# A fused H3 mixer and token MLP: one quarter of the sine table transposed earlier, and a new hand order behind the first shuffles

## The chip, the core and the metric

The kernel runs on one NeuronCore of a Trainium2 chip. The core has five engines that run side by side: TensorE (PE, matmuls and transposes into PSUM), ScalarE (ACT), VectorE (DVE), GpSimd (POOL) and SyncE (SP, which here only issues DMAs). 16 DMA engines move data between HBM and the on-chip memory and within it. The metric is the device time of one execution, in microseconds.

## What is computed

Two blocks follow each other on x = A_q (2048 rows of 448). Cut to what matters:

```
k_shift = sum over t of k_pad[:, t:t+S, :] * shift_k[:, 3-t]      # a filter of 4 taps
kv = k_shift * v
y  = irfft(rfft(kv, 2S) * rfft(ssm_k, 2S))[:S] + kv * ssm_D        # a long causal convolution
h  = x + layernorm(x) * y
u  = gelu(einsum("bsd,sf->bdf", layernorm(h), w1) + b1)            # an MLP along the sequence
h2 = h + (einsum("bdf,fs->bds", u, w2) + b2).transpose(0, 2, 1)
```

Inputs and output are bfloat16. S = 2048, D = 448, F = 1792.

## The kernel before

Every step is recorded first (`op(...)`: its engine, its function, what it reads and writes), with a name `step.number:k`. Nothing is planned at run time or by a heuristic: the strings in `ORDER` list, for each engine, all of its operations in the order in which they run, and `SLOTS` lists for every PSUM buffer which of the eight banks it takes and in which turn. `schedule()` replays these lists, and `emit()` writes the instructions with the semaphore waits that follow from data and buffers. An engine runs its list strictly in order, so an operation that waits holds up all that stand behind it.

The convolution is done as a transform of two stages with matmuls against tables of sines.

- `tables` builds the tables. `tables.5` and `tables.6` hold the phases of the halves h = 0 and h = 1 of the sine table E (DVE: L834, L838, L841) and their sine on ACT (L844). `tables.7` builds the small tables of stage 2 and of the inverse (sine L859 on ACT, products on POOL, L868). E has four quarters of eight 128x128 blocks.
- `kv` is the filter of 4 taps: transposes of k (L962), matmuls (L988), and the product with v (DVE, L1003). `kT` transposes the long filter ssm_k (L1034, evacuated at L738 by DVE); between its groups stand a few dummy matmuls (L1021), which compute nothing.
- `k1`, `u1` (`emit_stage1`) are stage 1 of the filter and of kv: for each of 16 pieces 8 matmuls (L1055), one evacuation of 128x896 (L1065 on ACT or DVE; for the first four pieces of k1 L1063 on DVE), and after every second piece three shuffles between partitions by DMA (L1071), one from SP and two from POOL. They go out of a ring of four buffers.
- `k2`, `u2` (`emit_stage2`) are stage 2 (L1090), evacuated by L736 and L739 (filter) or L735 and L738 (kv). `evac` is the helper of all evacuations: L735 and L736 are its lines on ACT, L738 and L739 on DVE.
- `i1` is the product of the two spectra (DVE, L1157) and the first stage of the inverse (L1174), in eight pairs of pieces, each with two evacuations (L735 or L738) and up to four shuffles by DMA (L1198; L1185 for the last pair). Names: `i1.1`, `i1.14`, `i1.8`, `i1.10`, `i1.12`, `i1.6`, `i1.4`, `i1.16` are the pairs in the order in which they run.
- `ct0` and `ct` transpose the sine table E for the second stage of the inverse: eight transposes per quarter (L1104) and one evacuation of 128x1024 into ET. `ct0.0` is quarter 0, and its `safter=i1_last[-1:]` names the last i1 matmul recorded so far, so it stands amid i1. `ct0.1` is a set of small DMAs on SP that need it: two fill rows with zeros (L1114), four copy rows of ET into a table EW (L1123). `ct.0` to `ct.2` are the other quarters, behind i1.
- `i2` is the second stage of the inverse (L1300 for two rows from EW, L1306), then the gate and the combination with x (ACT L1316, DVE L1318, L1326, L1336), and the second layer norm (ACT L1354, POOL L1364 to L1378, DVE L1385). `q` and `xn` are the first layer norm (DVE L1234, L1236; POOL L1242, L1245; ACT L1267).
- `warm` are single matmuls (L1208) without use for the result.
- `mlp` is the MLP: L1432 and L1442 with w1, the gelu (ACT L1422), L1454 with w2, and the last sum (DVE L1457). `w1a`, `w1b`, `w2` are its weight loads on SP (L1405, L1409, L1416); from the second on they wait until the i1 shuffles have landed.

Of the kernel before, what the change touches and what calls it, by code (L numbers as in the profile page):

```python
# [36 lines left out]
    ),  # L37
    "act": (
# [536 lines left out]
def _build(nc, A_q, A_k, A_v, A_shift_k, A_ssm_k, A_ssm_D, B_w1, B_b1, B_w2, B_b2, out):  # L575
# [33 lines left out]
    o_E = o_V + 14336  # L609
# [13 lines left out]
    o_IH = o_ID + 256  # L623
# [6 lines left out]
    with ctx:  # L630
# [395 lines left out]
        def emit_kT():  # L1026
            k = None
            for i, c in enumerate((0, 1, 2, 3)):
                cw = CW[c]
                for g in range(2):  # L1030
                    sch.t0 = T_KT + 1.0 * (2 * i + g)
                    b = _Buf(psum)
                    for rr in range(8):
# [3 lines left out]
                            safter=(k,) if c == 3 and rr == 0 else ())  # L1037
# [4 lines left out]
                if i < 3:  # L1042
                    dummy(N_WK, T_KT + 1.0 * (2 * i + 1), (k,))
# [100 lines left out]
        i1_last = []  # L1144
# [372 lines left out]
```

## Time and profile before

| | us |
|---|---|
| median of three runs | 171.09 |
| lowest and highest | 170.84, 171.63 |
| the profiled execution | 173.72 |
| its span, first to last instruction | 171.8 |

| engine | busy, us |
|---|---|
| PE | 162.3 |
| DVE | 101.7 |
| ACT | 90.5 |
| POOL | 59.7 |

The profile is of a single execution, and its times count from its first instruction. A row of the timeline gives the start, the length, the engine, the line, the operation, output and input with their shapes, and how many were merged; in brackets stands the idle time of the engine before it and what ended that. A row of the chain of work that ended last gives the start, the length, and the engine or transfer that the end hung on at that time. A row of a group of instructions gives the count, the busy time in us, the mean of one in ns, and the idle time before them. Rows with SPq and POOL of DMA_DIRECT2D show the issuing of a DMA, not the transfer.

### The profile page before, as it was taken

What the parts mean: (1) busy time and instruction counts of PE and PEld (TensorE: products, weight loads), DVE (VectorE), ACT (ScalarE), POOL (GpSimd) and SP (SyncE); (2) the same over time, 40 slices, a digit from 0 to 9 for tenths busy, and PEclk for the clock granted to TensorE, in tenths of its full rate; (3) what the DMA queues carried; (4) which work ended last, traced back from release to release, by engine and by line L of the source; (5) the groups of instructions that cost most, each with busy time, mean ns of one, the idle gap of its engine ahead of it and who ended that gap; (6) DMA issues with size and microseconds to landing.
All of it is one profiled execution on the core that took longest, in us unless ns stands there. A gap on an engine that the chain in (4) does not pass through costs nothing.

```text
span 171.8 us, 3572 instructions
## 1 busy us (share of the span) xinstructions
PE 162.3 (94%) x1419; PEld 94.5 (55%) x1419; DVE 101.7 (59%) x190; ACT 90.5 (53%) x131; POOL 59.7 (35%) x155
## 2 busy tenths in 40 slices
PE   6999999989988998959999999999999999999994
PEld 2786755443323343424544555555567777777783
DVE  7999998989999999948977830000003133132231
ACT  3696858999999999948875371203180000000000
POOL 8345727775910556752887370000000000000000
PEclk9999999999999999987999999999999999999999
DMA  5999798882849387658999999910000111101111
GB/s 161 414 342 369 228 299 327 341 322 110 255 106 391 100 232 203 185 147 276 387 398 402 424 422 421 420 67 0 0 0 4 53 53 53 53 0 57 53 53 53
DMA packets 15564, 35.15 MB, mean 205 GB/s; under 512 B 3804, under 2 KB 9644, under 8 KB 15548
## 3 DMA queue, kind: packets, MB, share of 16 engines
q1 hardware_dynamic: 12396, 28.26, 44.9%
q0 software_dynamic: 3008, 6.58, 12.5%
q8 instruction: 11, 0.18, 0.4%
q10 hardware_dynamic: 144, 0.08, 0.2%
q14 instruction: 5, 0.04, 0.1%
HBM read 22.05 MB, written 1.84 MB: 139 GB/s over the span
## 4 chain that ended last, share of the span: by engine, by line
PE 68%; ACT 21%; DMA 6%; DVE 2%; issue 2%; POOL 0%; DVEq 0%; ACTq 0%
PE ps L1454 24%; PE ps L1432 12%; PE ps L1442 12%; ACT arena L735 12%; DMA arena<-arena 6%; ACT arena L1065 6%; PE ps L1306 3%; PE ps L1055 3%; PE ps L1021 3%; ACT arena L736 3%; PE ps L962 3%; PE ps L1090 2%; PE ps L1034 2%; DVE arena L1336 1%; PE ps L988 1%
## 5 line engine op out<-in xcount | busy, mean ns | idle before, releaser
L1457 DVE SCALAR_TENSOR_TENSOR arena<-ps,arena 128x448 bf16<-128x448 f32 (+2 forms) x17 | 11.1, 656 | 55.3 <-PE ps L1454 55.3
L1454 PE MATMUL ps<-arena 128*128 128x448 bf16 (+2 forms) x238 | 42.7, 342 | 0.0
L1454 PEld LDWEIGHTS ps<-arena 128*128 128x128 bf16 x238 | 33.3, 145 | 9.5
L735 ACT CAST arena<-ps 128x896 bf16<-128x896 f32 (+1 forms) x30 | 23.8, 968 | 0.6 <-PE ps L931 0.4
L1432 PE MATMUL ps<-arena 128*128 128x448 bf16 x112 | 23.4, 353 | 0.1
L1065 ACT CAST arena<-ps 128x896 bf16<-128x896 f32 x25 | 21.0, 919 | 4.5 <-PE ps L1055 4.4
L1442 PE MATMUL ps<-arena 128*128 128x448 bf16 x112 | 22.2, 352 | 0.0
L1071 POOL DMA_DIRECT2D arena<-arena x32 | 17.6, 556 | 9.5 <-ACT arena L1065 8.3
L1422 ACT ACTIVATE arena<-ps,arena 128x448 bf16<-128x448 f32 x14 | 7.8, 641 | 18.3 <-PE ps L1442 14.6
L1090 PE MATMUL ps<-arena 128*64 128x448 bf16 x128 | 15.3, 359 | 2.2 <-ACT arena L735 0.7
L1432 PEld LDWEIGHTS ps<-arena 128*128 128x128 bf16 x112 | 10.8, 98 | 10.8 <-DVE arena L1385 0.9
L1157 DVE TENSOR_TENSOR arena<-arena 128x1792 bf16<-128x1792 bf16 x16 | 16.6, 1082 | 0.1
L1442 PEld LDWEIGHTS ps<-arena 128*128 128x128 bf16 x112 | 11.0, 98 | 10.2
L1055 PE MATMUL ps<-arena 128*32 128x448 bf16 x256 | 14.7, 356 | 0.5 <-ACT arena L1065 0.2
L1174 PE MATMUL ps<-arena 64*128 64x448 bf16 x128 | 13.7, 351 | 0.9 <-DVE arena L1157 0.6
L1198 POOL DMA_DIRECT2D arena<-arena x16 | 9.3, 585 | 14.5 <-ACT arena L735 11.9
L1090 PEld LDWEIGHTS ps<-arena 128*64 128x64 f16 x128 | 5.6, 108 | 11.3 <-ACT arena L735 4.5
L1385 DVE TENSOR_SCALAR arena<-arena 128x448 bf16<-128x448 f32 x16 | 7.9, 510 | 5.2 <-POOL arena L1378 5.1
L1306 PE MATMUL ps<-arena 128*128 128x448 bf16 x32 | 8.7, 395 | 2.0 <-DMA arena<-arena 2.0
L1174 PEld LDWEIGHTS ps<-arena 64*128 64x128 f16 x128 | 5.3, 94 | 8.8 <-DVE arena L1157 3.0
L1354 ACT ACTIVATE arena<-arena 128x448 bf16<-128x448 f32 x14 | 8.0, 573 | 4.0 <-DVE arena L1326 3.8
L1003 DVE TENSOR_TENSOR arena<-ps,arena 128x512 bf16<-128x512 f32 (+1 forms) x16 | 9.1, 614 | 1.0 <-PE ps L988 0.8
(99 smaller groups left out, 191.3 us busy)
## 6 DMA issues: line engine op xcount, KB each, us to landing
arena<-in_B_w_dram SPq DMA_DIRECT2D x8, 896.0 KB, 9.6
arena<-in_B_w_dram SPq DMA_DIRECT2D x2, 2048.0 KB, 17.4
arena<-arena SPq DMA_DIRECT2D x16, 224.0 KB, 3.8
arena<-arena POOLq DMA_DIRECT2D x32, 112.0 KB, 3.9
arena<-in_B_w_dram SPq DMA_DIRECT2D x2, 1536.0 KB, 19.3
arena<-arena POOLq DMA_DIRECT2D x13, 196.0 KB, 4.6
arena<-in_A_k_dram SPq DMA_DIRECT2D x4, 448.0 KB, 5.7
arena<-in_A_v_dram SPq DMA_DIRECT2D x4, 448.0 KB, 8.2
```

Of the source, the lines that this page charges most:

```text
L735: return e.copy(out=dst(), in_=src())
L1055: op("pe", lambda e, W, b=b, r=r, q=q, x=x, c0=c0: e.matmul(PS[32 * q:32 * q + 32, b.slots[x], 0:D], E[:, 2 * r + x, c0:c0 + 32], src[:, r ...
L1065: return e.copy(out=dst, in_=Ppair(b)) if W == "act" else e.tensor_copy(out=dst, in_=Ppair(b))
L1071: shuf[tag].append(op(q_, lambda e, W, g=g, i=i, a=a, nu=nu, jh=jh: e.dma_start(T[a + i:a + i + 4 * nu - 3:4].rearrange("p (j k) c d -> p ...
L1090: op("pe", lambda e, W, b=bs[h], h=h, j=j, c=c, par=par: e.matmul(PS[64 * par:64 * par + 64, b.slots[c], 0:D], FW[:, 64 * c:64 * c + 64], ...
L1157: op("dve", lambda e, W, m=m, i=i: e.tensor_tensor(out=MR(m.slots[0]).rearrange("p (x y) d -> p x y d", x=2), in0=TU[:, i].unsqueeze(2).br ...
L1174: k = op("pe", lambda e, W, b=bs[h], m=ms[h], par=par, t=t, tab=tab, xy=xy, P=P: e.matmul(Pb(b, par), tab[P, :], MR(m.slots[0])[P, xy, :], ...
L1306: k = op("pe", lambda e, W, b=b, r=r, h=h: e.matmul(Pb(b), ET[:, 2 * r + h, :], TZ[:, r, h, :], start=(h == 0 and r >= NZ), stop=(h == 1)) ...
L1432: op("pe", lambda e, W, r=r, fc=fc, b=bs[fc]: e.matmul(Pb(b), W1A[:, r, 128 * fc:128 * fc + 128], Q[:, r, :], start=(r == 0), stop=(r == R ...
L1442: op("pe", lambda e, W, r=r, fc=fc, b=b: e.matmul(Pb(b), W1B[:, r, 128 * (fc - n0):128 * (fc - n0) + 128], Q[:, r, :], start=(r == 0), sto ...
L1454: op("pe", lambda e, W, r=r, fc=fc, b=b, d0=d0, d1=d1: e.matmul(Pb(b)[:, d0:d1], W2[fc // 7][:, fc % 7, r:S:R], G[:, fc, d0:d1], start=(fc ...
L1457: op("dve", lambda e, W, r=r, b=b, A=A, d0=d0, d1=d1: e.scalar_tensor_tensor(out=XR(r)[:, d0:d1], in0=Pb(b)[:, d0:d1], scalar=bm[:, r:r + ...
```

## The change

The transposes of quarter 0 lose the edge to the last i1 matmul, so the order may put them anywhere behind the sine. They now stand amid the transposes of ssm_k (`kT`), in the place of three dummy matmuls, and are evacuated by ACT instead of DVE; on ACT the sine of the half h = 0 goes ahead of that of h = 1, and the copy goes ahead of the small sine of `tables.7`. The strings for all engines are new from there on: up to the first shuffles of k1 they differ in little, behind them in much. On SP the four copies into EW (`ct0.1:2` to `ct0.1:5`) stand ahead of all i1 shuffles, and both zero fills ahead of the loads of x. A number of evacuations change between ACT and DVE, and most PSUM buffers get another bank. The computed result is the same.

```
                 for i in range(8):
                     op("pe", lambda e, W, b=b, h=h, i=i: e.transpose(
...
-                       r=[...], bw=[b], kind="tr", safter=i1_last[-1:])
+                       r=[...], bw=[b], kind="tr", safter=i1_last[-1:] if late else ())
...
-                if i < 3:
+                if i < 2:
                     dummy(N_WK, T_KT + 1.0 * (2 * i + 1), (k,))
...
     "pe":
-        "... kT.2:0-3 kT.3:9-11 kT.5:0-7 kT.2:4-7 kT.5:9-10 kT.6:0-7 kT.7:0-7 bias.0:0 kT.5:11 kv.7:0-7 k1.8:0-7 "
+        "... kT.2:0-3 kT.3:9-11 kT.5:0-7 kT.2:4-7 ct0.0:0-7 kT.6:0-7 kT.7:0-7 bias.0:0 kv.7:0-7 k1.8:0-7 ..."
...
-        "... u1.2:0-7 u1.3:0-7 kv.13:8-27 u1.4:0-7 k1.5:0-7 kv.14:0-23 k1.6:0-7 u1.5:0-7 k1.2:0-7 k1.7:0-7 ..."
+        "... u1.2:0-7 u1.3:0-7 u1.4:0-7 kv.13:0-27 k1.5:0-7 k1.6:0-7 kv.14:0-23 k1.7:0-7 k1.2:0-7 u1.5:0-7 ..."
...
-        "... u2.10:0-3 i1.1:1-8 i1.14:10-17 i1.1:10-17 i1.14:1-8 i1.8:1-8 i1.10:1-8 i1.8:10-17 i1.10:10-17 u2.4:0-3 u2.5:0-3 ct0.0:0-7 i1.12:1-8 ..."
+        "... i1.1:1-8 i1.1:10-17 u2.10:0-3 i1.14:1-8 i1.14:10-17 i1.10:1-8 i1.8:1-8 i1.8:10-17 u2.4:0-3 u2.5:0-3 i1.10:10-17 ..."
...
-        "i1.16:1-8 ct.0:0-7 ct.1:0-7 i2.1:0-3 warm.0:0 i2.9:0-3 i2.2:0-1 i2.10:0-1 ct.2:0-7 warm.1:0 i2.45:0-1 ..."
+        "i1.16:1-8 ct.0:0-7 warm.0:0 i2.1:0-3 ct.1:0-7 i2.9:0-3 i2.2:0-1 i2.10:0-1 ct.2:0-7 i2.45:0-1 ... i2.32:0-1 warm.1:0 "
...
     "act":
-        "tables.0:5 kv.4:12 kv.3:8 kv.6:12 tables.6:3 tables.5:3 tables.7:5 bias.0:1 k1.8:8 ..."
+        "tables.0:5 kv.4:12 kv.3:8 kv.6:12 tables.5:3 tables.6:3 ct0.0:8 bias.0:1 tables.7:5 k1.8:8 ..."
...
-        "... u1.0:8 u1.1:8 u1.2:8 u1.3:8 u1.4:8 k1.5:8 k1.6:8 u1.5:8 k1.7:8 ..."
+        "... u1.0:8 u1.1:8 u1.2:8 u1.4:8 k1.5:8 k1.6:8 k1.7:8 u1.5:8 ..."
...
     "dve":
-        "... i1.0:0 i1.14:0 i1.1:0 i1.7:0 i1.13:0 i1.9:0 i1.8:0 i1.10:0 i1.11:0 i1.10:9 i1.12:0 ct0.0:8 i1.5:0 ..."
+        "... i1.0:0 i1.1:0 i1.13:0 i1.14:0 i1.9:0 i1.7:0 i1.8:0 i1.10:0 i1.12:0 i1.11:0 i1.10:18 ... i1.5:0 i1.6:0 i1.3:0 i1.6:9 ..."
...
     "sp":
-        "u1.11:11 u1.15:11 ct0.1:0 xload.2:0 xload.3:0 w1a.0:0 ct0.1:1 i1.1:20 i1.1:22 i1.14:20 i1.14:22 i1.8:20 "
-        "i1.8:22 i1.10:20 i1.10:22 ct0.1:2 ct0.1:4 i1.12:20 i1.12:22 ct0.1:3 ct0.1:5 i1.6:22 i1.4:18 i1.16:21 "
-        "i1.16:19 w1a.1:0 ..."
+        "u1.11:11 u1.15:11 ct0.1:0-1 xload.2:0 xload.3:0 w1a.0:0 ct0.1:2 ct0.1:4 ct0.1:3 ct0.1:5 i1.1:20 i1.1:22 "
+        "i1.14:20 i1.14:22 i1.8:20 i1.8:22 i1.10:20 i1.10:22 i1.12:20 i1.12:22 i1.6:22 i1.4:18 i1.16:21 i1.16:19 "
+        "w1a.1:0 ..."
```

In these strings `...` stands for names that are left out. In a group of i1 such as `i1.10`, `:1-8` and `:10-17` are the matmuls of its two halves, `:9` and `:18` their evacuations, and the numbers from 19 on its shuffles.

More of the change, by code (lines that the diff above doesn't have):

```diff
@@ L1105, in emit_ct @@
                         out=Pbf(b, 0, f16)[:, 128 * i:128 * i + 128], in_=E[:, 8 * h + i, :], identity=IH),
-                       r=[(o_E + 2048 * h + 256 * i, 256), (o_IH, 256)], bw=[b], kind="tr", safter=i1_last[-1:])
+                       r=[(o_E + 2048 * h + 256 * i, 256), (o_IH, 256)], bw=[b], kind="tr", safter=i1_last[-1:] if late else ())
                 evac(lambda h=h: ET[:, 8 * h:8 * h + 8, :].rearrange("p a b -> p (a b)"),
```

134 rows, old and new, of tables (ORDER, SLOTS) are left out of this document.

## The prediction

> **What bounds the kernel now.** I read the engine shares first, then the table of stages, then the chain of work that ended last.
>
> ```profile
> PE 162.3 (94%) x1419; PEld 94.5 (55%) x1419; DVE 101.7 (59%) x190; ACT 90.5 (53%) x131; POOL 59.7 (35%) x155
> ...
> PE 68%; ACT 21%; DMA 6%; DVE 2%; issue 2%; POOL 0%; DVEq 0%; ACTq 0%
> ```
> ```profile
> 30.00:40.00 10.00, 8.81 (x152) 4.54 (x148) 9.32 (x19) 9.45 (x13) 6.97 (x14) 1.00 0.88 332
> 40.00:50.00 10.00, 9.25 (x106) 3.20 (x100) 9.81 (x16) 9.61 (x12) 6.68 (x15) 1.00 0.49 142
> 50.00:60.00 10.00, 9.18 (x88) 3.26 (x85) 9.95 (x11) 10.00 (x14) 2.39 (x4) 1.00 0.66 222
> 60.00:70.00 10.00, 9.33 (x92) 3.93 (x92) 9.87 (x12) 10.00 (x13) 5.27 (x10) 1.00 0.80 217
> ...
> 75.40:81.40 6.00, 5.89 (x28) 3.00 (x28) 4.64 (x14) 3.30 (x6) 1.24 (x3) 0.72 0.61 197
> 81.40:127.00 45.60, 45.60 (x240) 23.38 (x241) 16.39 (x47) 21.17 (x48) 15.09 (x38) 1.00 0.70 279
> ```
> ```profile
> 66.95 2.45 ACT arena L735 x3
> 69.40 0.04 issue
> 69.44 0.81 ACT arena L735
> 70.25 5.13 DMA arena<-arena
> ...
> 75.42 1.48 PE ps L1306 x4
> ...
> 82.51 0.38 PE ps L1306 x2
> ...
> 126.83 42.08 PE ps L1454 x231
> ```
>
> The share of 94% for PE is misleading. In the table (window, length, then busy time of PE, weight loads, DVE, ACT and POOL, granted clock, DMA share, GB/s) PE is really full only from 81.4 us on: 45.60 of 45.60, then the 42.08 us of the last chain row. None of the products there is removed, so the change is worth exactly what it moves the point at 81.4. Ahead of it, from 50 to 70 us, ACT is busy 10.00 of 10.00 twice and DVE 9.95 and 9.87. They empty PSUM and form the products of the spectra. The chain agrees: ACT evacuations up to 70.25, then 5.13 us of a shuffle through the DMA engines, and only then the first matmul that reads the shuffled rows.
>
> **The transposes of quarter 0 (ct0.0), early.** They leave the full stage and go among the filter's transposes.
>
> ```profile
> 7.20 1.22 DVE L841 TENSOR_SCALAR arena<-arena 128x2048 int32<-128x2048 int32 x1
> ...
> 11.71 0.54 PE L1021 MATMUL ps<-arena 128*128 128x448 bf16 x2
> ...
> 35.10 1.70 PE L1090 MATMUL ps<-arena 128*64 128x448 bf16 x16 [0.59 <-ACT arena L1065]
> ...
> 60.47 0.62 PE L1104 MATMUL ps<-arena 128*128 128x128 f16 x8
> ```
> ```profile
> 8.72 3.91 ACT L844 ACTIVATE arena<-arena 128x2048 f16<-128x2048 int32 x2
> 12.53 0.61 ACT L859 ACTIVATE arena<-arena 128x384 f32<-128x384 int32 x1
> 13.51 0.17 ACT L735 CAST arena<-ps 128x14 f32<-128x14 bf16 x1 [0.38 <-PE ps L931]
> 14.76 1.71 ACT L1065 CAST arena<-ps 128x896 bf16<-128x896 f32 x2 [1.08 <-PE ps L1055]
> ```
>
> Can the input be late? The two sines (L844) change places, so that the half with quarter 0 comes first. Its argument is ready when the second L841 ends, at 7.20 + 1.22 = 8.42 us, and ACT starts its first sine at 8.72 anyway. So the first sine ends near 8.72 + 3.91/2 = 10.7 us, and PE arrives at the new place at about 11.7. No wait. On PE, eight transposes (0.62 us as a burst at the old place) replace three dummy matmuls, two of which take 0.54 us here: about 0 us. On ACT the copy of 128x1024 is a new piece of about 0.9 to 1.0 us between the sines and L859. ACT has 0.38 + 1.08 = 1.46 us idle between the bias and the first evacuation at 14.76, so this fits, with about 0.5 us over. Without that cover the first four evacuations would slip by up to 1.0 us. What stands behind it, the small sine L859 and POOL's tables made from it, comes some 1 us later; stage 2 (L1090), which reads them, starts at 35.10. I cost the early part at 0, between 0 and +0.5.
>
> **The evacuations between 18 and 71 us.** Of the evacuations that carry 896 columns, seven go from ACT to DVE (u1.3, u1.15, one each of k2.1, u2.1, u2.13, i1.10, i1.6) and six from DVE to ACT (u1.11, one each of k2.1, k2.15, u2.1, i1.10, i1.12): ACT has one less, DVE one more, and DVE loses the copy of quarter 0.
>
> ```profile
> L735 ACT CAST arena<-ps 128x896 bf16<-128x896 f32 x29 | 23.6, 996 | 0.2 <-PE ps L1090 0.2
> ...
> L739 DVE TENSOR_SCALAR arena<-ps 128x896 bf16<-128x896 f32 x7 | 7.3, 1082 | 0.7 <-PE ps L1090 0.7
> ...
> L738 DVE COPY arena<-ps 128x1024 f16<-128x1024 f16 x1 | 0.7, 692 | 0.1
> ```
>
> In a stream an ACT evacuation costs 23.6/29 = 0.81 us, a DVE one 7.3/7 = 1.04, the copy 0.69. So ACT: -0.81. DVE: +1.04 - 0.69 = +0.35. DVE's idle time from 30 to 70 us is 0.68 + 0.19 + 0.05 + 0.13 = 1.05, which can take the 0.35 if it lies in the right places; if all of it can be used, the end moves by -0.81, and if none, DVE is the longer one and the end moves by +0.35. Shared evenly over both engines it is (0.35 - 0.81)/2 = -0.23. ACT is the engine in the chain, so I take a value on its side of the middle: **-0.4**, with both ends kept. PE loses 0.62 us of transposes at 60 us, where it is busy 9.33 of 10 and waits for the other two: 0.
>
> The rest of the reordering (kv.13 behind u1.4, each i1 pair finished before the next is begun) changes who waits within the stage and removes no work. Its first shuffles leave earlier, but the later pairs set the end. It is inside the bounds above.
>
> **SP's queue.** The four small copies into EW (L1123) no longer stand between the i1 shuffles; they go ahead of all of them, behind the zero fill and the loads.
>
> ```profile
> 64.11 1.66 SPq L1123 DMA_DIRECT2D arena<-arena  x2
> 65.86 1.41 SPq L1198 DMA_DIRECT2D arena<-arena  x2
> 67.32 2.16 SPq L1123 DMA_DIRECT2D arena<-arena  x2
> 69.52 1.43 SPq L1198 DMA_DIRECT2D arena<-arena  x2
> 70.99 1.39 SPq L1185 DMA_DIRECT2D arena<-arena  x2
> 76.81 1.47 SPq L1405 DMA_DIRECT2D arena<-in_B_w_dram  x3
> ```
> ```profile
> 65.35 5.94 ACT L735 CAST arena<-ps 128x896 bf16<-128x896 f32 x7
> ```
> ```profile
> 69.93 1.15 POOL L1198 DMA_DIRECT2D arena<-arena  x2 [1.54 <-ACT arena L735]
> 71.07 0.61 POOL L1185 DMA_DIRECT2D arena<-arena  x1
> 71.67 0.55 POOL L1198 DMA_DIRECT2D arena<-arena  x1
> 72.21 0.61 POOL L1185 DMA_DIRECT2D arena<-arena  x1
> ```
>
> The pair of L1123 at 67.32 holds SP until 69.48, and from there SP issues four shuffles back to back, one each 0.7 us. The second of them (near 70.23) belongs to the same pair as POOL's at 69.93, so it is at least 0.3 us late. ACT's last evacuation ends at 65.35 + 5.94 = 71.29, and SP's last shuffle goes out near 70.99 + 0.70 = 71.7: 0.4 us late. These delays go. But POOL's last, at 72.21, is the later one of the two, it is not behind L1123, and the weight load that waits for the shuffles starts at 76.81. So of 0.4 us I take **-0.1** (bounds 0 and -0.4). Moving the copies forward puts the first i1 shuffles of SP behind them; those carry the two last rows, which nothing reads before 75 us, so I cost that at 0.
>
> The Trainium skill speaks against more than this ("DMA: Bandwidth & Descriptors", section "Issuing engines are not separate DMA queues"): copies started by any engine run on the same 16 DMA engines, so another issuer saves only issue time. By it the freed SP is worth the 0.4 us of issue at most, and nothing of the 5.13 us.
>
> **Sum.** 0 - 0.4 - 0.1 = -0.5 us. The profiled execution took 173.72 us, 171.8 of it the span and 1.9 around it; it becomes 173.2. The median of the runs, 171.09, lies 2.6 below the profiled one; I subtract the same 0.5 there: **170.6 us**.
>
> Part of those 2.6 us is the clock: 0.72 from 75.4 to 81.4 us means (1 - 0.72) x 6.0/0.5 = 3.4 us at half speed, and four matmuls took 1.48 us at 75.42, where two take 0.38 later. The change has the same gap ahead of them, so I count no difference. The Trainium skill's "TensorE: Matmul & The Clock Gate" (Part 1, "What's actually happening") states half clock after an idle window of about 3.4 us whose phase is free; the 3.4 us here agree, and a kernel could therefore show the dip in one run and not in another.
>
> **Rivals.**
> *More than the sum.* The whole ACT evacuation is gained and SP's lateness too: -0.81 - 0.41 = -1.2, 169.9 us. For it: the second line of the first fence, where ACT has 21% of the chain and DVE 2%. Against it: DVE is as full as ACT.
> *DVE becomes the bound.* The change does not do what it says: the copy leaves, but a longer evacuation comes, and ten products in a row hold up others. +0.35 - 0.1 = about +0.2, 171.3 us. For it 9.95 and 9.87 of 10.00; against it the 1.05 us of idle time.
> *The last shuffles crowd each other (slower).* SP's and POOL's last shuffles now leave closer together.
>
> ```profile
> arena<-arena POOLq DMA_DIRECT2D x2, 196.0 KB, 5.7
> ```
> ```profile
> arena<-arena POOLq DMA_DIRECT2D x1, 98.0 KB, 4.6
> arena<-arena POOLq DMA_DIRECT2D x1, 28.0 KB, 4.5
> ```
>
> The first row is of the issues at 61.4 us, where SP and POOL issue as fast as they can: 5.7 us to landing. The others are of the last ones, near 72 us: 4.6. If the end gets as crowded, the last landing comes 5.7 - 4.6 = 1.1 us later; if the pair before it, which the first matmul behind the gap reads, is stretched as well, up to twice that. In the middle it is +1.65, less the 0.4 of the evacuations: +1.2, 172.3 us (bounds 171.8 and 172.9). It decides as soon as the last shuffle takes more than 5.0 us, and ends beyond 171.95 when it takes some 5.9. For it: the DMA share is 0.80 from 60 to 70 us. Against it: the bytes are the same and the first pairs leave earlier.
>
> **How the numbers follow.** Chances: the sum 0.40, more than the sum 0.31, DVE 0.11, crowding 0.18. Half a per cent, about what a measurement of this kernel can tell from no change, is 0.86 us: faster means below 170.23, slower above 171.95. The sum and DVE lie within; of the sum 0.03 may reach below 170.23. Of the crowding 0.03 lies under 171.95, and about as much comes from an early slip (+0.5) met with DVE's +0.35. That gives faster 0.34, same 0.48, slower 0.18. The forecast's own range is 170.2 to 171.0; the range for eight in ten goes from 169.6 (a little beyond the full gain) to 172.0 (the lower part of the crowding).
>
> **What would show it.** Right: the copy of 128x1024 on ACT ends before 14.3 us and the first L1065 stays near 14.7; ACT's last evacuation ahead of the late transposes ends at 70.9 instead of 71.29; SP issues its last shuffle within 0.1 us of that; the last POOL shuffle goes out near 71.8 and takes about 4.6 us; the back-to-back stretch begins 0.5 us earlier than 81.4. Wrong: DVE without any idle time and ACT waiting in the stage; a last landing of 5.5 us or more; or a start of the stretch that moves because the granted clock dips in one of the two profiles and not in the other.

## The result and the profile after

| | before | changed |
|---|---|---|
| median of the runs | 171.92 us (170.84 to 172.84, 20 runs) | 171.02 us (170.21 to 171.78, 20 runs) |
| profiled execution | 173.72 us, span 171.8 | 171.1 us, span 169.1 |

The ratio is 0.9941, 95% interval [0.9924, 0.9959]: some 1.0 us faster, where 0.5 was forecast. In this series the kernel before took 171.92 us, in the three runs shown ahead of the prediction, the first of these 20, 171.09, so only the ratio is to be compared.

The two profiled executions differ by more than the medians, 2.6 us. The first rows to read are therefore span and mean granted clock, of the execution shown before and of a second profile of the same unchanged kernel (`before_again` below):

```profile
core 0: 171.8 us, clock 0.988
```
```profile
core 0: 169.9 us, clock 1.000
```

The execution shown before was a rare one. Of 95 other runs of that kernel one had a clock as low (0.990, 174.12 us), and all others 0.998 or more. PE's gap ahead of `i2.2`, the first matmul that needs the late shuffles, was longer in it as well, 2.01 us where the second profile has 0.95:

```profile
75.42 1.48 PE L1306 MATMUL ps<-arena 128*128 128x448 bf16 x4 [2.01 <-DMA arena<-arena]
```
```profile
74.43 0.93 PE L1306 MATMUL ps<-arena 128*128 128x448 bf16 x4 [0.95 <-DMA arena<-arena]
```

From here on the second profile stands for the kernel before. Its chain of waits, start and length in us:

```profile
70.11 4.27 DMA arena<-arena
74.38 0.05 issue
74.43 0.93 PE ps L1306 x4
75.36 0.24 PE ps L1104 x4
75.62 0.68 DVE arena L1336
76.29 0.55 DVE arena L1342
76.84 0.93 PE ps L1306 x4
...
79.72 1.12 PE ps L1432 x5
...
124.98 42.09 PE ps L1454 x231
```

The changed kernel, same view:

```profile
71.52 4.20 DMA arena<-arena
75.77 2.82 PE ps L1306 x14
...
124.11 42.09 PE ps L1454 x231
```

In the old chain the end hangs on a shuffle issued at 70.11. It is SP's half of the seventh pair (`i1.4:18`; the expectations below count from 0 and call it the sixth), not one of the last pair: the first matmul behind the gap (`i2.2`, 74.43) needs it, and behind that matmul a product (L1336) and its statistics (L1342) on DVE hold up the next rows until 76.84. By the trace's records of DMA the last shuffle of all landed shortly before, at 76.64, and it was SP's; POOL's last landed at 75.94. In the new chain it hangs on POOL's last shuffle, issued at 71.52. PE's own rows of the changed kernel there:

```profile
73.52 0.92 PE L1306 MATMUL ps<-arena 128*128 128x448 bf16 x4 [0.61 <-issue]
74.27 0.61 PE L1104 MATMUL ps<-arena 128*128 128x128 f16 x8
75.77 1.50 PE L1306 MATMUL ps<-arena 128*128 128x448 bf16 x7 [0.89 <-DMA arena<-arena]
...
78.67 1.12 PE L1432 MATMUL ps<-arena 128*128 128x448 bf16 x5
```

`i2.2` comes 0.9 us sooner than in the kernel before (0.4 us when both are counted from the last evacuation), PE then waits for the transfer and not for DVE, and from 75.77 on it runs without a gap.

The table of stages of the changed kernel (window, length, busy time of PE, weight loads, DVE, ACT and POOL, granted clock, DMA share, GB/s):

```profile
30.00:40.00 10.00, 9.33 (x152) 4.32 (x156) 9.90 (x18) 9.12 (x11) 6.84 (x13) 1.00 0.85 316
40.00:50.00 10.00, 9.12 (x104) 3.11 (x96) 9.61 (x14) 9.78 (x13) 6.17 (x14) 1.00 0.52 145
50.00:60.00 10.00, 9.39 (x86) 3.18 (x84) 9.96 (x10) 10.00 (x14) 2.87 (x5) 1.00 0.81 266
60.00:70.00 10.00, 9.29 (x90) 3.58 (x87) 9.78 (x17) 9.95 (x14) 5.48 (x11) 1.00 0.64 197
...
78.70:124.30 45.60, 45.60 (x241) 23.38 (x241) 16.55 (x47) 21.70 (x48) 14.02 (x38) 1.00 0.74 293
```

The stretch is as full as before (45.60 of 45.60, then 42.09), and ACT is as full from 50 to 70 us as it was. The DMA share has turned round: 0.66 and 0.80 before from 50 and from 60 us, now 0.81 and 0.64. The transfers come earlier.

ACT's last evacuations, before (second profile) and now:

```profile
63.71 7.53 ACT L735 CAST arena<-ps 128x896 bf16<-128x896 f32 x9
```
```profile
12.27 0.99 ACT L735 COPY arena<-ps 128x1024 f16<-128x1024 f16 x1
...
14.18 1.71 ACT L1065 CAST arena<-ps 128x896 bf16<-128x896 f32 x2 [0.33 <-PE ps L1055]
...
63.18 7.53 ACT L735 CAST arena<-ps 128x896 bf16<-128x896 f32 x9
```

They end at 71.24 and at 70.71. From there to the stretch it takes 79.72 - 71.24 = 8.48 us and 78.67 - 70.71 = 7.96 us. So of the 1.05 us between the two starts of the stretch 0.53 lie ahead of the last evacuation and 0.52 behind it. (From its start to the first L1454 the stretch takes 45.26 us before and 45.44 now, so 0.87 of the 1.05 us reach the end.) Of the first part only 0.18 can be put down to the change: from the first evacuation of `k2.3` (43.66 and 43.32) to the end of the last one it takes 27.58 and 27.40 us, and the place where that begins scatters from 43.3 to 44.2 over eleven profiles, with no order by kernel. The rows of ACT there, before (second profile) and now, show one wait for PE fewer:

```profile
45.67 1.76 ACT L736 ACTIVATE arena<-ps 128x896 bf16<-128x896 f32 x2 [0.20 <-PE ps L1090]
47.62 0.91 ACT L735 CAST arena<-ps 128x896 bf16<-128x896 f32 x1 [0.19 <-PE ps L1090]
```
```profile
45.33 2.54 ACT L736 ACTIVATE arena<-ps 128x896 bf16<-128x896 f32 x3 [0.23 <-PE ps L1090]
47.75 0.91 ACT L735 CAST arena<-ps 128x896 bf16<-128x896 f32 x1
```

SP's issues in the changed kernel:

```profile
50.78 2.68 SPq L1123 DMA_DIRECT2D arena<-arena  x4
54.39 15.26 SPq L1198 DMA_DIRECT2D arena<-arena  x12
69.79 1.62 SPq L1185 DMA_DIRECT2D arena<-arena  x2
```

The four copies (L1123) are through before the first shuffle, and SP ends its last issue at 71.41, 0.7 us after the last evacuation: it issues without delay and is no longer in the chain, which is POOL's.

### The profile page after: what moved, and what is told of

The parts are those of the page before. It is cut to its first block, busy times and chain, and to the rows that moved or that the text cites. A ratio compares the mean times of both kernels' runs of the same rounds, so it can differ in the third digit from the quotient of the medians.

```text
span 169.1 us, 3564 instructions
## 1 busy us (share of the span) xinstructions
PE 160.0 (95%) x1416; PEld 92.3 (55%) x1416; DVE 101.9 (60%) x191; ACT 90.5 (54%) x130; POOL 58.5 (35%) x155
## 4 chain that ended last, share of the span: by engine, by line
PE 64%; ACT 19%; DMA 5%; DVE 4%; POOL 4%; issue 2%; DVEq 0%; ACTq 0%; POOLq 0%
PE ps L1454 25%; PE ps L1432 13%; PE ps L1442 13%; ACT arena L735 12%; DMA arena<-arena 5%; ACT arena L736 4%; ACT arena L1065 4%; PE ps L1306 3%; PE ps L1055 3%; PE ps L1034 2%; PE ps L988 2%; PE ps L1090 2%; POOL arena L1071 2%; DVE arena L834 1%; PE ps L962 1%
## 5 line engine op out<-in xcount | busy, mean ns | idle before, releaser
L1454 PE MATMUL ps<-arena 128*128 128x448 bf16 (+2 forms) x238 | 42.7, 342 | 0.0
L1454 PEld LDWEIGHTS ps<-arena 128*128 128x128 bf16 x238 | 33.3, 145 | 9.5
L1432 PE MATMUL ps<-arena 128*128 128x448 bf16 x112 | 23.5, 353 | 0.0
L735 ACT CAST arena<-ps 128x896 bf16<-128x896 f32 (+1 forms) x29 | 23.1, 937 | 0.0
L1065 ACT CAST arena<-ps 128x896 bf16<-128x896 f32 x24 | 20.3, 914 | 4.7 <-PE ps L1055 4.2
L1442 PE MATMUL ps<-arena 128*128 128x448 bf16 x112 | 22.3, 352 | 0.0
L1198 POOL DMA_DIRECT2D arena<-arena x16 | 9.3, 583 | 13.9 <-ACT arena L735 12.9
L1234 DVE BATCH_NORM_STATS2 arena<-arena 128x6 f32<-128x448 bf16 x16 | 9.4, 612 | 0.6 <-DMA arena<-in_A_q_dram 0.6
L1055 PEld LDWEIGHTS ps<-arena 128*32 128x32 f16 x256 | 5.0, 95 | 8.2 <-ACT arena L1065 2.2
```

The lines of the kernel that those rows point to most:

```text
L735: return e.copy(out=dst(), in_=src())
L1055: op("pe", lambda e, W, b=b, r=r, q=q, x=x, c0=c0: e.matmul(PS[32 * q:32 * q + 32, b.slots[x], 0:D], E[:, 2 * r + x, c0:c0 + 32], src[:, r ...
L1065: return e.copy(out=dst, in_=Ppair(b)) if W == "act" else e.tensor_copy(out=dst, in_=Ppair(b))
L1234: op("dve", lambda e, W, bs=bs, r=r: e.bn_stats(out=bs, in_=XR(r)), r=[(oX(r), DB)], w=[(ob, 24)], n=D, kind="1x")
L1432: op("pe", lambda e, W, r=r, fc=fc, b=bs[fc]: e.matmul(Pb(b), W1A[:, r, 128 * fc:128 * fc + 128], Q[:, r, :], start=(r == 0), stop=(r == R ...
L1442: op("pe", lambda e, W, r=r, fc=fc, b=b: e.matmul(Pb(b), W1B[:, r, 128 * (fc - n0):128 * (fc - n0) + 128], Q[:, r, :], start=(r == 0), sto ...
```

## The experiments

Ratios are against the kernel before, run on the same chip in the same series (its medians there: 171.78, 171.90 and 172.01 us). "Back" is the order from matmul `k2.2` on, "front" what stands ahead of it behind the transposes of quarter 0. The last two columns come from one profile each: the longest landing of the shuffles that POOL issues at L1198, and the time from the end of the last evacuation to the stretch. The first four rows come from one series and the last three from another. Two profiles of the changed kernel differ by 0.23 us in the last column (7.96 above, 7.73 here), so a difference of that size tells nothing there.

| kernel | ct0.0 | SP's order | front | back | median us (runs) | ratio | longest landing | to the stretch |
|---|---|---|---|---|---|---|---|---|
| before_again | late | old | old | old | 172.07 (12) | 1.0010 [0.9983, 1.0037] | 5.7 | 8.48 |
| ct0_early | early | old | old | old | 171.61 (12) | 0.9996 [0.9968, 1.0025] | 6.0 | 8.21 |
| ct0_early_sp | early | new | old | old | 171.42 (12) | 0.9970 [0.9941, 0.9998] | 5.6 | 7.79 |
| new_order_old_sp | early | old | new | new | 170.94 (12) | 0.9948 [0.9919, 0.9977] | 4.3 | 7.49 |
| new_back_only | early | new | old | new | 170.74 (10) | 0.9935 [0.9912, 0.9959] | 4.6 | 7.56 |
| new_front_only | early | new | new | old | 171.03 (12) | 0.9956 [0.9936, 0.9976] | 5.8 | 7.95 |
| changed_again | early | new | new | new | 170.86 (10) | 0.9948 [0.9930, 0.9966] | 4.4 | 7.73 |

**The kernel before, once more.**

> The kernel before, unchanged, to see its granted clock run by run. Clock theory (its half-speed dip near 75 us is what the change removes): a good part of the runs show a mean clock of 0.99 or less, and those are about 1 us longer than the others. Shuffle theory (the gain is in the shuffles that land earlier): the clock is 1.00 in nearly all runs, as in the changed kernel, and the span of such runs lies about 1.0 us above the changed kernel's.

The stretch began at 79.72 at full clock, and nearly every run of the unchanged kernel was without a dip. That the change removes a dip falls as a cause.

**Quarter 0 early, and nothing else.**

```
-                       r=[...], bw=[b], kind="tr", safter=i1_last[-1:])
+                       r=[...], bw=[b], kind="tr", safter=i1_last[-1:] if late else ())
...
pe:  -kT.5:9-11                          +ct0.0:0-7 ahead of kT.6:0
act: -tables.6:3 tables.5:3 tables.7:5 bias.0:1    +tables.5:3 tables.6:3 ct0.0:8 bias.0:1 tables.7:5
dve: -ct0.0:8
```

> The kernel before with quarter 0 alone moved: transposes amid those of ssm_k, copy on ACT, nothing else reordered, SP's order as before. Evacuation theory (the full ACT and DVE stage is what got shorter): -0.3 to -0.6 us, since DVE loses its 0.69 us copy. Shuffle theory: -0.2 to +0.1 us, since SP still issues the four copies into EW between the i1 shuffles.

By the runs nothing, 0.9996, but the interval reaches down to what the evacuation theory expected. The trace decides: from `k2.3` to the end of the last evacuation it took 27.56 us instead of 27.58, although DVE no longer has the copy. The evacuation stage is not shortened by that copy.

**SP's new order as well.**

```
sp: -... i1.10:22 ct0.1:2 ct0.1:4 i1.12:20 i1.12:22 ct0.1:3 ct0.1:5 i1.6:22 ...
    +... w1a.0:0 ct0.1:2 ct0.1:4 ct0.1:3 ct0.1:5 i1.1:20 i1.1:22 ...
```

> As ct0_early, and SP's order from the changed kernel: the four copies into EW ahead of all i1 shuffles, both zero fills ahead of the loads of x. Shuffle theory: at least 0.5 us faster than ct0_early, -0.6 to -1.0 us in all, with SP's last large shuffle landing at least 1 us earlier against the last evacuation. Evacuation theory: no more than 0.1 us faster than ct0_early.

By the medians 0.2 us, by the ratios 0.4 against `ct0_early`; the intervals overlap, so if it is a gain it is a small one. By the values neither theory was met: the one asked for 0.5 us at least, the other for no more than 0.1. The chain of `ct0_early`, with the old SP, still goes through the seventh pair's shuffle:

```profile
70.17 4.47 DMA arena<-arena
74.64 0.05 issue
74.69 0.93 PE ps L1306 x4
```

With the new SP order that shuffle went out at 69.85 and landed after 3.35 us by the trace's records of DMA, at 73.20. But POOL's half of the same pair landed at 74.21, so `i2.2` came at 74.30: the other half of the pair took over the wait after 0.4 us. So SP's half did land 1.5 us earlier, counted from the last evacuation, but it was not alone in holding up `i2.2`.

**The changed kernel with SP's old order.**

```
sp: the string of before, all else as changed
```

> The changed kernel with SP's order of before: the four copies into EW between the i1 shuffles again. Shuffle theory: most of the gain goes, -0.4 to +0.1 us against the kernel before. Evacuation theory: -0.7 to -1.0 us, as the changed kernel.

The version of the shuffle theory that rested on SP's queue alone falls: 0.9948, as good as the changed kernel. The time is the one that the evacuation theory expected, but its stage was only 0.17 us shorter than in `ct0_early` (27.39 and 27.56), and the stretch began 0.7 us sooner after it (7.49 and 8.21). The rows of SP show why the copies did no harm.

```profile
63.70 1.35 SPq L1123 DMA_DIRECT2D arena<-arena  x2
65.10 1.41 SPq L1198 DMA_DIRECT2D arena<-arena  x2
66.55 1.34 SPq L1123 DMA_DIRECT2D arena<-arena  x2
67.99 2.51 SPq L1198 DMA_DIRECT2D arena<-arena  x2
```

The copies (L1123) still stand between the shuffles, but the pairs ahead of them now leave earlier, and SP is through with the copies at 67.89. The shuffle at 67.99 is done with at some 68.7, and the seventh pair's goes out as soon as its evacuation is ready (69.81). SP's half then took 3.31 us to land, as with the copies moved. By the ratios the copies cost some 0.3% behind the old pairs, with intervals that overlap, and nothing that can be told behind the new ones.

**Front and back taken apart.** What remained was the order itself. In the new back, the first i1 pair is evacuated ahead of `u2.11`, and each pair is finished before the next is begun. The back also holds a new order of the transposes `ct`, of i2 and of the MLP, which no run takes apart from the pairs.

```
act, old back: u2.7:4 u2.11:5 u2.11:4 i1.1:9 u2.7:5 i1.1:18 i1.14:18 i1.14:9 i1.8:9 i1.8:18 i1.10:18 ...
act, new back: u2.7:4-5 i1.1:9 i1.1:18 u2.11:4 i1.14:9 i1.14:18 u2.11:5 i1.8:9 i1.8:18 i1.10:9 ...
```

> The kernel before with quarter 0 early, SP's new order, and the changed kernel's order from the second last group of the k2 stage (matmul k2.2) on; the k1 and u1 stages keep the old order. Spacing theory (the last half microsecond of the gain comes because the first pair of the i1 stage is evacuated ahead of the last evacuations of the u2 stage, so that the shuffles leave earlier and further apart and land sooner): first shuffle issued 11.1 us after the start of the evacuation stage rather than 13.0; large shuffles 3.8 to 3.9 us in the mean, those of pair 3 (i1.10) 2.5 to 4.2 us; median 171.0 to 171.2, like the changed kernel. Rival, the front order (k1, u1 and the first part of k2): shuffles as above or not, but median 171.4 as with quarter 0 early and SP's new order alone.

> The changed kernel with the old order from matmul k2.2 on (quarter 0 early and SP's new order kept). Spacing theory: pair 3's shuffles 5.5 to 6 us again, large shuffles 4.4 us in the mean, median 171.4 to 171.5. Front rival: 171.0 to 171.1, with the shuffles as slow as before.

> The changed kernel as it is, on the same chip as the three others: 171.0 (170.8 to 171.2), large shuffles 3.8 to 3.9 us in the mean, stretch 7.5 to 8.0 us after the last evacuation.

The shuffles follow the back, as the spacing theory has it. The shuffles of L1198 in the kernel before, `new_front_only` and `new_back_only` (first and last start, then the landing times):

```profile
L1198 POOL DMA_DIRECT2D arena<-arena x16: 545/587/623, 56.9 to 71.6; - x16
...
DMA to landing us min/median/max: 3.1/4.3/5.7
```
```profile
L1198 POOL DMA_DIRECT2D arena<-arena x16: 542/587/623, 56.7 to 71.4; - x16
...
DMA to landing us min/median/max: 3.1/4.5/5.8
```
```profile
L1198 POOL DMA_DIRECT2D arena<-arena x16: 545/587/623, 54.8 to 71.2; - x16
...
DMA to landing us min/median/max: 3.2/4.0/4.6
```

With the new back the first goes out 2 us earlier, the last at about the same time, and the longest landing falls from 5.7 or 5.8 to 4.6 us. The issues of 61.3 to 62.7 us are where the two differ most, first with the old back (kernel before), then with the new one (changed kernel):

```profile
arena<-arena POOLq DMA_DIRECT2D x3, 196.0 KB, 5.7
```
```profile
arena<-arena POOLq DMA_DIRECT2D x2, 196.0 KB, 3.9
```

So the shuffles in the middle land sooner with the new back. The late ones of POOL do not: its last large one (98 KB) took 3.8 us in the kernel before and 4.2 and 4.0 in the two profiles of the changed one. The late ones of SP do, but for that either SP's new order or the new order of the others was enough: by the trace's records SP's half of the seventh pair took 4.27 us in the kernel before and 4.47 in `ct0_early`, and 3.2 to 3.4 in all the others of the table; SP's last shuffle took 5.07 and 4.54, and 3.7 to 4.3.

The times tell less. `new_back_only` is like the changed kernel, as expected. `new_front_only` should have stayed at 171.4 to 171.5 us and took 171.03, the rival's number, with slow shuffles: the spacing theory missed there. With the old back and SP's new order the ratios are 0.9970 and 0.9956, with the new back 0.9935, 0.9941 and 0.9948: the back is worth some 0.2% on top of SP's order, but each interval is about as wide as that. The profiles show 0.16 us of it in the evacuation stage (27.55 us in `new_front_only`, 27.39 in `new_back_only`) and nothing sure behind it (7.95 in `new_front_only`, 7.56 to 7.96 with the new back). A value for the new front can't be told from nothing: -0.14% with the old back, +0.1% with the new one.

**The two 28 KB shuffles of the seventh pair last on POOL.**

```
pool: -i1.4:20-21 i1.16:22 i1.4:19 i1.16:20        +i1.4:20 i1.16:22 i1.16:20 i1.4:21 i1.4:19
```

> The changed kernel with one difference in POOL's queue: the two 28 KB shuffles of the sixth pair behind the last two large ones. If the last landing of a large shuffle sets the start of the back-to-back stretch: POOL's last large shuffle is issued 0.1 us after the last evacuation ends rather than 0.8, the last large one lands 0.4 to 0.7 us sooner, the stretch begins 0.25 to 0.5 us sooner, median 170.5 to 170.8. If VectorE's chain on the first two output rows sets it as much: at most 0.1 us, median 170.9 to 171.0.

The last landing did come sooner, 4.4 us after the last evacuation instead of 4.8 to 5.0, but the time stayed: 170.89 us (170.46 to 172.49, 12 runs), 0.9957 [0.9930, 0.9983]. In its profile the stretch began no sooner, 8.25 us after the last evacuation. PE's rows in that profile, and the landing of POOL's half of the seventh pair:

```profile
74.62 0.92 PE L1306 MATMUL ps<-arena 128*128 128x448 bf16 x4 [1.19 <-issue]
...
75.82 0.54 PE L1306 MATMUL ps<-arena 128*128 128x448 bf16 x2
76.53 0.55 PE L1306 MATMUL ps<-arena 128*128 128x448 bf16 x2 [0.17 <-DVE arena L1336]
```
```profile
arena<-arena POOLq DMA_DIRECT2D x1, 196.0 KB, 4.8
```

That half took 4.8 us where it took 4.2 in both profiles of the changed kernel. `i2.2` came at 74.62, and PE then waited for DVE's product of the first rows (L1336). So two landings set the start between them: the seventh pair's, through `i2.2` and DVE, and the last pair's. Here the first took over.

**One shuffle of the seventh pair from POOL to SP.**

```
-        QZ = {(2, 0): ("pool", "pool"), (1, 0): ("sp", "pool"), (1, 1): ("pool", "pool")}
+        QZ = {(2, 0): ("pool", "pool"), (1, 0): ("sp", "pool"), (1, 1): ("sp", "pool")}
pool: -i1.4:20-21 i1.16:22 i1.4:19 i1.16:20        +i1.4:21 i1.16:22 i1.16:20 i1.4:19
sp:   i1.4:20 behind i1.4:18
```

> The changed kernel with one large shuffle of the sixth pair (i1.4, second half) issued by SP, right behind the other, rather than by POOL, and POOL's last large shuffle ahead of the last 28 KB one. Reading of the run with the 28 KB shuffles put last: two landings set the stretch's start between them, this shuffle (matmul i2.2 waits for it, and VectorE's two products behind i2.2 free the bank for the rows that follow) and the last large one of the last pair. If both are so and SP's shuffles land in 3.3 to 3.7 us as its others do: i2.2 0.1 to 0.2 us sooner after the last evacuation (2.6 to 2.7 us rather than 2.8), the last large landing 4.3 to 4.5 us after it rather than 4.8 to 5.0, the stretch 7.4 to 7.6 us after it rather than 7.7 to 8.0, and a median of 170.5 to 170.8. If the DMA engines are loaded so that one shuffle's gain is another's loss: i2.2 or the last landing comes later by as much, and the median stays at 170.9 to 171.1.

170.92 us (170.33 to 171.99, 12 runs), 0.9931 [0.9900, 0.9963]: no better than the changed kernel. Its chain:

```profile
70.39 3.94 DMA arena<-arena
74.34 0.05 issue
74.38 0.93 PE ps L1306 x4
```

The shuffle goes out behind the other one, at 70.39, lands after 3.94 us instead of 4.2, and `i2.2` is no sooner (3.0 us after the last evacuation, 2.8 in the changed kernel): it was issued 1.0 us ahead of the end of the last evacuation, POOL's 1.5. POOL's last large landing came 4.3 us after the last evacuation instead of 4.8 to 5.0, and SP's last, behind one shuffle more, after 4.7 instead of 3.7 to 3.8. One transfer's gain was another's delay. The rule of the Trainium skill that was quoted in the prediction ("DMA: Bandwidth & Descriptors", section "Issuing engines are not separate DMA queues") speaks for that outcome, and the time of this run agrees with it. The run is no test of the rule alone, since the time to landing differs between the two issuers as well (last section). No version here beats the changed kernel by more than the intervals.

## Why the prediction was half right

**Quarter 0 early, 0 us: right.** The copy on ACT ends at 12.27 + 0.99 = 13.26 us, ahead of 14.3, and the first L1065 is not late (14.18). Alone the edit gives 0.9996.

**Evacuation stage, -0.4 us: mis-sized, from a wrong place.** It became 0.18 us shorter, and that comes with the new back alone (27.39 us in `new_back_only`, 27.55 in `new_front_only`). The step that failed is the count "ACT has one less". The -0.81 was taken over all evacuations from 18 to 71 us and set against a stage that is full only from 50 on. Counted from `k2.2` on, four evacuations leave ACT (u2.13, u2.1, i1.10, i1.6) and four come (k2.15, u2.1, i1.10, i1.12). The one that is missing lies in u1, ahead of 43 us, where ACT had idle time. What the runs showed in its place is the one wait for PE fewer. That DVE lost the copy of quarter 0 was worth 0.02 us in `ct0_early`.

**The order of the i1 pairs, "removes no work. Its first shuffles leave earlier, but the later pairs set the end": wrong.** This was left inside the bounds of another term, and the new order, front and back together, carries the gain even without SP's (0.9948 in `new_order_old_sp`). The later pairs do set the end, but how long SP's late shuffles take depends on what stands ahead of them. A transfer's 5.13 us was taken as given: it was 4.27 and 4.47 in the two other profiles with SP's and the other engines' old orders, and 3.2 to 3.4 where either was new. That the earlier pairs leave the DMA engines freer is the likely reason; it is argued from the landing times, and no run varies the spacing alone.

**SP's queue, -0.1 us: too small, for a reason that the rows quoted would have shown.** I priced the lateness of SP's last shuffle and found POOL's later. That goes by the issues; by the landings SP's was the later one in the second profile, 76.64 against 75.94 (76.62 against 76.80 in the first). The chain quoted at the start named another: the 5.13 us from 70.25 on begin with SP's shuffle of the seventh pair. Against the old back the new SP order gave 0.2 to 0.4 us (0.9996 to 0.9970, with intervals that overlap). "Nothing of the 5.13 us" was wrong too: by the trace's records SP's shuffle of the seventh pair took 4.27 and 4.47 us behind the copies, and 3.35 with the copies moved. With the new order SP's gives nothing that can be told: counted from `ct0_early`, it is 0.3% alone, the new order of the other engines 0.5% alone, both 0.5 to 0.6%. Either of them shortens SP's late landings, so the two are not to be added.

**The sum.** The forecast of -0.5 us had the larger part in the evacuations and the smaller in the shuffles; by the profiles it is the other way, 0.18 us and 0.5 or more. That the total stayed within a factor of two owes something to luck, since one term was too large and the other too small.

**Rivals.** *More than the sum* (-1.2) was nearest in size, but by shuffles, not evacuations. *DVE as the bound* did not come: its busy time from 60 to 70 us fell from 9.87 to 9.78. *Crowding* did not decide: POOL's last shuffle took 4.20 us, under the 5.0 from which that rival was to decide. Against the second profile of the kernel before, where it took 3.77, it was a little slower.

**The clock, no difference counted: right for the medians.** The comparison of the two profiles alone would have told 2.6 us, most of it the dip. So the sign that the prediction named, a start of the stretch that moves because the clock dips in one profile alone, did come true for the first pair of profiles. That a dip may show in one run and not in another was so, though more seldom than the prediction let one think: one run in 95. "The same gap" was not the same: 2.01 us in the profile with the dip, 0.95 and later 0.85 in the one without, 0.61 and later 0.89 in the changed kernel. Whether the longer gap brought on the dip is not shown.

What stays open: how the 1.0 us divides between the back and SP's order to better than 0.2 us, what the back and the front are worth each with SP's old order, what the new order of `ct`, i2 and the MLP adds, why POOL's 196 KB shuffle took 4.8 instead of 4.2 us in `pool_small_last` (one profile), and whether the new front is worth anything.

## What to carry to other kernels

Where a chain hangs on a transfer, find by its time of issue which transfer it is, and which instruction reads it; the last one issued need not be the one that counts. A transfer's time is no constant to be carried over a reordering: here the ones in the middle and SP's late ones landed faster when the earlier ones were issued sooner and further apart, POOL's late ones did not. Where several late transfers end close together, count the landing of each, since the next one takes over the wait. Before an evacuation saved on an engine is booked as gain, count the moves within the stage in which that engine is full.

## What the runs showed of the hardware

A 196 KB shuffle of the same pattern, issued by POOL, landed after 3.1 us as the first of its stage and after up to 6.0 us amid others. Issued over 16.4 us instead of 14.7, in another order, POOL's sixteen shuffles of that line took 4.6 us at most. In one and the same profile of the changed kernel, SP's 196 KB half of the seventh pair landed 3.25 us after its issue and POOL's, issued 0.26 us later, after 4.18; why is not shown. And a dip of the granted clock that one profile of a kernel shows (0.988) was absent from 94 of 95 other runs of it (0.998 or more): a single profile made the kernel before look 1.9 us longer than the next one.
